# Sharing PSUM by single banks and pairs, with gates on ScalarE and new paces, in a planned attention and FFN kernel

## Chip, core and metric

One core of a Trainium2 chip runs the whole kernel in one launch. The metric is the device time of one execution in microseconds (us). The engines are TensorE (PE in the profile), VectorE (DVE), ScalarE (ACT), GpSimd (POOL) and SyncE (SP), which issues nearly all DMAs here. Each runs its own instructions in order and waits on semaphores for the others.

## What is computed

```python
def _A_ref(x, wqkv, w_phi, wo):                    # x: 1 x 2048 x 640, 32 heads of 20
    qkv = (x @ wqkv).reshape(B, S, 3, H, Dh).transpose(2, 0, 3, 1, 4)
    q, k, v = qkv[0], qkv[1], qkv[2]
    pq = einsum("bhsd,hdf->bhsf", q, w_phi)
    pk = einsum("bhsd,hdf->bhsf", k, w_phi)
    phi_q = concatenate([softmax(pq), softmax(-pq)], axis=-1)
    phi_k = concatenate([softmax(pk), softmax(-pk)], axis=-1)
    kv = einsum("bhsf,bhsd->bhfd", phi_k, v)
    z  = einsum("bhsf->bhf", phi_k)
    o  = einsum("bhqf,bhfd->bhqd", phi_q, kv) / (einsum("bhqf,bhf->bhq", phi_q, z) + 1e-6)
    return o.transpose(0, 2, 1, 3).reshape(B, S, D) @ wo
def _B_ref(x, w_gate, w_up, w_down):               # inner width 1728
    return (silu(x @ w_gate) * (x @ w_up)) @ w_down
g = sigmoid((x * gate_w).sum(-1, keepdims=True))
out = g * _A_ref(x, ...) + (1 - g) * _B_ref(x, ...)
```

All data are bf16. The attention is linear, so keys and values of all 2048 tokens must be summed before the first query tile can be finished.

## The kernel before

The 2048 tokens are 16 tiles of 128 (index `t`) in 4 batches of 512 (index `bt`). Work is cut into tasks, each for one engine.

- **Premultiply** (`premult`, task `pre`): the feature weights are folded into the key and query weights, in five pieces each. A piece is six small matmuls into two PSUM banks, and ACT or DVE copies it to `wqk` (L722 on DVE, the helper L412 on ACT).
- **Values and gates** (`vtile`, tasks `v`, `vcp`, `gtan`): one tile of values with one more column, the gate's logit. ACT copies the values and takes a tanh of half the logit into `gtan`. After every fourth tile the task `gs` makes `gs[:, 0]` = 0.5 gtan + 0.5 and `gs[:, 1]` = 0.5 - 0.5 gtan for the four tiles, with two TENSOR_SCALAR on DVE (L755, L757).
- **Features** (`features`; `p1` for keys through `ktile`, `p0` for queries through `qtile`): 10 matmuls into two banks. Then come the row maximum (L799), the minimum (L803) and two subtractions (L807, L811) on DVE, the Exp on ACT, sums (L822) and reciprocal (L826) on DVE, and the normalisation on POOL (L832). The banks are free behind L811. The pool `pp` lets two such tiles hold PSUM at a time.
- **Key-value sums** (`kvpart`): per batch two halves, each into one bank, added up on DVE.
- **Query tiles** (`qtile`): the features are transposed by DMA, multiplied with the sums (`num`), divided (`den`, L914, and `o`), transposed by DMA again and multiplied with `wo`.
- **FFN** (`ffn`, `ffn_tail`, `ffn_head`): for each block `k` of 128 inner columns and each batch, 5 matmuls `gate` and 5 `up` of 512 columns. ACT makes a tanh of the gate's half and a copy of the up part (`us`), DVE combines tanh and gate (`stt`, L579), and POOL multiplies by the up part (`hmul`, L585). Block 13 is half as wide and has both parts in one bank. `down` then takes 28 matmuls for a tile; it needs all 14 blocks of its batch.
- **Output** (`finish`, `finals`): the branch that comes first is scaled by its gate into `xsb`, the other is scaled and added, and SP stores the tile.

The order of instructions is not written by hand. `_Plan.run` is a list scheduler that runs when the kernel is built: for each engine it takes, at the modelled time, the first task by priority whose dependencies have ended, whose earliest time (`hold`) has come and whose buffers are free. What it emits is fixed, and the chip executes it in that order. Keys have priority 3, values 4, queries 5 and FFN blocks and `down` 10 and up (a smaller number goes first), so the FFN fills what the attention leaves. The costs that it plans with stand in the `add` calls (0.75 us for L799, L803, L807 and L811, 1.44 for L822, 0.47 for L826, 0.59 for L579, and 0.08 more between dependent instructions of one engine).

PSUM has 8 banks of 512 fp32 columns. Before, the plan hands them out as four pairs (`"ps": 4`), for every task alike: an FFN block holds a pair from its first matmul until `stt` is done, and a half of the key-value sums or the warm-up holds a pair of which it uses one bank.

The paces: key tile `t` starts no earlier than 26.0 + 6.19 t, query tile `t` no earlier than 120.1 + 8.21 t, and piece `m` of the key weights no earlier than 21.4 + 1.1 m (all us on the plan's clock). `D_AFTER` says behind how many FFN blocks of the next batch the first `down` of a batch is put in the priorities.

Of the kernel before, what the change touches and what calls it, by code (L numbers as in the profile page):

```python
# [6 lines left out]
P = 128  # L7
# [7 lines left out]
NK = 14  # L15
# [191 lines left out]
class _Task:  # L207
    __slots__ = ("eng", "cost", "lat", "fn", "deps", "prio", "acq", "rel", "end", "seq", "name", "stop", "after", "land", "hold", "slack")
# [20 lines left out]
class _Plan:  # L229
# [16 lines left out]

    def run(self):
        left = {e: [] for e in self.LAT}
        for t in sorted(self.tasks, key=lambda t: (t.prio, t.seq)):
            left[t.eng].append(t)  # L250
        busy = {e: 0.8 for e in self.LAT}
        releases = []
        now = 0.0
        n = len(self.tasks)
        times = {0.8} | {t.hold for t in self.tasks if t.hold > 0.8}
        while n:
            if not times:
                names = [t.name for e in left for t in left[e]][:12]
                raise RuntimeError("plan is stuck: %s" % names)
            now = min(times)  # L260
            times.discard(now)
            for r in [r for r in releases if r[0] <= now]:
                releases.remove(r)
                self.free[r[1]].append(r[2])
                self.free[r[1]].sort()
# [37 lines left out]
def _build(  # L303
# [75 lines left out]
    plan = _Plan({"ps": 4, "phi": NPHI, "st": 3, "eT": 2, "ob": 2, "oT": 2, "us": 3, "dn": 2, "xb": 2, "pp": 2})  # L379
    add = plan.add  # L380

    def bank(i, j, c0, c1, r0=0, r1=P):
        return ps[r0:r1, (2 * i + j) * 512 + c0:(2 * i + j) * 512 + c1]

# [158 lines left out]
    def warm():  # L543
        z = us[:, 0, :]
        mms(acc(bank(wctx["ps"], 1, 0, 512), [(us[:, 0, 0:P], z)] * 9))
    warm_t = add("pe", 3.84, warm, deps=[zero], prio=-10, acq=[("ps", wctx, "ps")], rel=[("ps", wctx, "ps")], name="warm")


# [11 lines left out]
    def ffn_tail(bt, k, ctx, last, n_after):  # L560
        hb = bt % 2
        rows = P if k < 13 else 64
        hap = hT[0:rows, hb, k, :]

        def gap():
            return bank(ctx["ps"], 0, 0, 512, 0, rows)

        def uap():
            return bank(ctx["ps"], 1, 0, 512) if k < 13 else bank(ctx["ps"], 0, 0, 512, 64, P)
# [12 lines left out]

        def mult():
            u_ = usa()
            poolop(lambda: pool.tensor_tensor(hap, hap, u_, ALU.mult), [hap, u_], [hap])  # L585
        mult_t[bt, k] = add("pool", 1.11, mult, deps=[t2, t3], prio=0, rel=[("us", ctx, "us")], name="hmul")

    def ffn(bt, k, rank):
# [4 lines left out]
        if k == 13:  # L593
            one = add("pe", _mm(*[512] * 5), lambda: mms(acc(bank(ctx["ps"], 0, 0, 512),
                      [(wg[:, c, 1664:1792], xT[:, c, tsl]) for c in range(5)])),
                      deps=before + [xl[bt], wgl[NPC], wul[NPC]], prio=rank, acq=[("ps", ctx, "ps")], name="gu")
            ffn_tail(bt, k, ctx, (one, one), 0)
            return
        g_ = add("pe", _mm(*[512] * 5), lambda: mms(acc(bank(ctx["ps"], 0, 0, 512),
                 [(wg[:, c, P * k:P * k + P], xT[:, c, tsl]) for c in range(5)])),  # L600
                 deps=before + [xl[bt], wgl[w_]], prio=rank, acq=[("ps", ctx, "ps")], name="gate")
        u_ = add("pe", _mm(*[512] * 5), lambda: mms(acc(bank(ctx["ps"], 1, 0, 512),
                 [(wu[:, c, P * k:P * k + P], xT[:, c, tsl]) for c in range(5)])),
                 deps=[wul[w_]], prio=0.0, name="up")
# [3 lines left out]
    def ffn_head():  # L608
# [4 lines left out]
        for c0, c1 in ((0, 2), (2, 4), (4, 5)):  # L613
            for j, (w, wl) in enumerate(((wg, wgl), (wu, wul))):
                def fn(c0=c0, c1=c1, j=j, w=w):
                    mms([(bank(cs[k]["ps"], j, 0, 512), w[:, c, P * k:P * k + P], xT[:, c, tsl], c == 0, c == 4)
                         for c in range(c0, c1) for k in range(2)])
                last = add("pe", _mm(*[512] * (2 * (c1 - c0))), fn, deps=[xs[0][c1 - 1], wl[0]], prio=-5,
                           acq=[("ps", cs[0], "ps"), ("ps", cs[1], "ps")] if c0 == 0 and j == 0 else (), name="head")
# [18 lines left out]
    def finish(t, which, ctx, dep):  # L638
        sc = gs[:, 0 if which == "a" else 1, t:t + 1]
        x_ = xsb[:, t, :]  # L640
        rel = [("ps", ctx, "ps")]
# [34 lines left out]
    def down(bt, u, rank):  # L676
# [8 lines left out]
        hold = {"deps": [mult_t[bt, k] for k in range(NK)] + wd_l, "prio": rank, "acq": [("ps", ctx, "ps")], "name": "down"}  # L685
# [12 lines left out]
    def premult(which, wT_l, prio, step=0.0, at=0.0):  # L698
        ev = []
        for m in range(5):  # L700
# [14 lines left out]
            t1 = add("pe", 0.4, fn, deps=[wT_l] + wbd_t, prio=prio + step * m, acq=[("ps", ctx, "ps")], name="pre")  # L715
            t1.hold = at + 1.1 * m if at else 0.0

            def ev_fn(m=m, ctx=ctx):
# [4 lines left out]
                else:  # L723
                    actop(o_, i_, ACTF.Copy)
            ev.append(add("dve" if which and m % 2 else "act", 0.73 if which and m % 2 else 0.6, ev_fn, deps=[t1], prio=-1,
                          rel=[("ps", ctx, "ps")], name="prev"))
# [6 lines left out]
    def vtile(t, prio):  # L733
# [6 lines left out]
        def fn():  # L740
# [3 lines left out]
                 acq=[("ps", ctx, "ps")], name="v")  # L744
# [4 lines left out]
                 deps=[c_], prio=0.4, rel=[("ps", ctx, "ps")], name="gtan")  # L749
        v_t[t] = c_  # L750
        if t % 4 == 3:
            q = slice(4 * bt, 4 * bt + 4)

            def gsf():
                dveop(lambda: dve.tensor_scalar(gs[:, 0, q], gtan[:, q], 0.5, 0.5, op0=ALU.mult, op1=ALU.add),  # L755
                      [gtan[:, q]], [gs[:, 0, q]])
                dveop(lambda: dve.tensor_scalar(gs[:, 1, q], gtan[:, q], -0.5, 0.5, op0=ALU.mult, op1=ALU.add),  # L757
                      [gtan[:, q]], [gs[:, 1, q]])
            gs_t[bt] = add("dve", 0.3, gsf, deps=[g_], prio=2, name="gs")
# [7 lines left out]
    def features(t, which, wq_l, prio, ctx):  # L767
# [6 lines left out]
        def fn():  # L774
# [4 lines left out]
                 acq=[("ps", ctx, "ps"), ("phi", ctx, "phi"), ("st", ctx, "st"), ("pp", ctx, "pp")], name="p" + str(which))  # L779
# [36 lines left out]
        a4 = add("dve", 0.75, f_sn, deps=[a2, a3], prio=age, rel=[("ps", ctx, "ps"), ("pp", ctx, "pp")], name="sub")  # L816
# [16 lines left out]
        b1 = add("dve", 1.44, f_sm, deps=[x1], prio=age, name="sum")  # L833
# [9 lines left out]
    def kvpart(bt, half, prio):  # L843
# [4 lines left out]
        def fn():  # L848
            grp = []
            for g in range(g0, g1):  # L850
                c0, c1 = WIN * g, min(WIN * g + WIN, VW)
                o_ = bank(ctx["ps"], 0, c0 - WIN * g0, c1 - WIN * g0)
                for i in range(4):
# [4 lines left out]
                 prio=prio, acq=[("ps", ctx, "ps")],  # L858
# [6 lines left out]
        p_ = lambda: bank(ctx["ps"], 0, 0, v1_ - v0)  # L865
# [14 lines left out]
        if bt < NBT - 1:  # L880
            kva_t[half] = add("dve", 0.48, evac, deps=[m_, kva_t.get(half)], prio=1.5, rel=[("ps", ctx, "ps")], name="kva")
# [3 lines left out]
        else:  # L885
            kvs_t[half] = add("dve", 0.95, masked, deps=[m_, kva_t[half]] + mask_t, prio=1.4, rel=[("ps", ctx, "ps")], name="kvs")
# [3 lines left out]
    def qtile(t, prio):  # L890
# [34 lines left out]
        d2 = add("dve", 0.73, f_o, deps=[d1], prio=1.2, rel=[("ps", c2, "ps"), ("dn", c2, "dn")], name="o")  # L925
# [9 lines left out]
        a_ = add("pe", _mm(*([512] * 5 + [128] * 5)), wof, deps=[tO, wo_l], prio=1.5, acq=[("ps", c3, "ps")],  # L935
# [90 lines left out]
```

## Time and profile before

| | |
|---|---|
| median of 3 runs | 292.12 us (291.95 to 292.25) |
| profiled execution | 291.88 us |
| its span, first to last instruction | 289.7 us |
| granted TensorE clock | 1.000 |
| busy: PE, DVE, POOL, ACT | 281.7, 226.0, 166.9, 145.1 us |
| HBM read, written | 8.30 MB, 2.62 MB |

The page divides the span into 40 slices and gives each engine's busy share in tenths. It follows the chain of work that ended last backwards from the last instruction. Other views list instructions in order of time, with the idle time of the engine just before each and what ended it, or give the busy time in chosen stretches. Matmuls overlap in the pipeline, so one row's duration is longer than the distance to the next row. Some matmul records are missing in a trace; weight loads (PEld) are all there: 2065 of them stand against 2027 matmul records here.

### The profile page before, as it was taken

What the parts mean: (1) busy time and instruction counts of PE and PEld (TensorE: products, weight loads), DVE (VectorE), ACT (ScalarE), POOL (GpSimd) and SP (SyncE); (2) the same over time, 40 slices, a digit from 0 to 9 for tenths busy, and PEclk for the clock granted to TensorE, in tenths of its full rate; (3) what the DMA queues carried; (4) which work ended last, traced back from release to release, by engine and by line L of the source; (5) the groups of instructions that cost most, each with busy time, mean ns of one, the idle gap of its engine ahead of it and who ended that gap; (6) DMA issues with size and microseconds to landing.
All of it is one profiled execution on the core that took longest, in us unless ns stands there. A gap on an engine that the chain in (4) does not pass through costs nothing.

```text
span 289.7 us, 5139 instructions
## 1 busy us (share of the span) xinstructions
PE 281.7 (97%) x2027; PEld 151.7 (52%) x2065; DVE 226.0 (78%) x325; ACT 145.1 (50%) x214; POOL 166.9 (58%) x131
## 2 busy tenths in 40 slices
PE   7999998999999999999999999999999999999996
PEld 2445554555555446555655555555455555445554
DVE  1234798999899998989999887888998987872112
ACT  2546465665865744444463634555665455564110
POOL 5396134576575467574377575787697455666100
PEclk9999999999999999999999999999999999999999
DMA  8999998000000000000053444523443533322211
GB/s 181 226 230 323 248 267 265 1 5 0 2 0 2 0 2 0 2 0 0 2 101 75 94 97 96 111 65 85 75 79 68 118 76 73 72 46 52 70 45 45
DMA packets 65415, 23.90 MB, mean 82 GB/s; under 512 B 53936, under 2 KB 65392, under 8 KB 65392
## 3 DMA queue, kind: packets, MB, share of 16 engines
q1 hardware_dynamic: 64736, 23.58, 36.0%
q8 instruction: 16, 0.26, 0.4%
q10 hardware_dynamic: 656, 0.00, 0.1%
q14 instruction: 7, 0.06, 0.1%
HBM read 8.30 MB, written 2.62 MB: 38 GB/s over the span
## 4 chain that ended last, share of the span: by engine, by line
PE 85%; DVE 5%; POOL 3%; SPq 2%; issue 2%; DMA 1%; ACT 1%; ACTq 0%; POOLq 0%
PE ps L402 85%; SPq L430 2%; POOL hT L585 2%; DMA wph<-in_A_w_phi_dram 1%; DVE sm L822 1%; DVE mx L799 1%; DVE phi L807 1%; DVE phi L811 1%; DVE mn L803 1%; POOL wbd L520 1%; POOL wbd L523 1%; DVE gs L755 0%; POOL wbd L519 0%; ACT wqk L412 0%; ACT us L412 0%
## 5 line engine op out<-in xcount | busy, mean ns | idle before, releaser
L832 POOL TENSOR_TENSOR phi<-phi,rc 128x1320 bf16<-128x1320 bf16 x32 | 77.6, 2426 | 48.0 <-DVE rc L826 47.9
L585 POOL TENSOR_TENSOR hT<-hT,us 128x512 bf16<-128x512 bf16 (+1 forms) x56 | 64.2, 1155 | 35.7 <-DVE hT L579 30.2
L402 PE MATMUL ps<-xT,wg 128*128 128x512 bf16 x268 | 67.0, 379 | 0.9 <-ACT wqk L412 0.3
L402 PE MATMUL ps<-xT,wu 128*128 128x512 bf16 x254 | 64.3, 379 | 0.7 <-DMA wu<-in_B_w_up_dram 0.3
L402 PE MATMUL ps<-wd,hT 128*128 128x128 bf16 (+1 forms) x441 | 61.9, 298 | 0.4
L822 DVE TENSOR_REDUCE sm<-phi 128x66 f32<-128x1320 bf16 x32 | 48.7, 1521 | 11.5 <-ACT phi L412 11.2
L412 ACT ACTIVATE hT<-ps 128x512 bf16<-128x512 f32 (+1 forms) x56 | 33.2, 595 | 40.5 <-PE ps L402 40.4
L412 ACT ACTIVATE phi<-phi 128x1320 bf16<-128x1320 bf16 x32 | 41.6, 1301 | 23.1 <-DVE phi L811 23.0
L579 DVE SCALAR_TENSOR_TENSOR hT<-hT,ps 128x512 bf16<-128x512 bf16 (+1 forms) x56 | 37.5, 674 | 19.3 <-ACT hT L412 19.3
L402 PE MATMUL ps<-wqk,xT 128*128 128x512 bf16 (+2 forms) x315 | 48.0, 299 | 1.6 <-DVE phi L811 1.3
L402 PEld LDWEIGHTS ps<-wd,hT 128*128 128x128 bf16 x448 | 35.0, 98 | 27.4
L402 PEld LDWEIGHTS ps<-xT,wu 128*128 128x128 bf16 x260 | 25.4, 98 | 31.2 <-DMA wu<-in_B_w_up_dram 0.8
L412 ACT ACTIVATE us<-ps 128x512 bf16<-128x512 f32 (+1 forms) x56 | 33.3, 596 | 16.4 <-PE ps L402 14.9
L402 PEld LDWEIGHTS ps<-xT,wg 128*128 128x128 bf16 x280 | 25.5, 98 | 26.8 <-issue 0.9
L402 PEld LDWEIGHTS ps<-wqk,xT 128*128 128x128 bf16 x320 | 26.5, 98 | 23.2 <-DVE phi L811 1.5
L799 DVE TENSOR_REDUCE mx<-ps 128x33 f32<-128x660 f32 x32 | 26.3, 822 | 4.1 <-PE ps L402 3.7
L811 DVE TENSOR_TENSOR phi<-mn,ps 128x660 bf16<-128x660 f32 x32 | 26.5, 829 | 0.6
L803 DVE TENSOR_REDUCE mn<-ps 128x33 f32<-128x660 f32 x32 | 26.4, 824 | 0.0
L807 DVE TENSOR_TENSOR phi<-ps,mx 128x660 bf16<-128x660 f32 x32 | 26.2, 819 | 0.0
L671 POOL TENSOR_TENSOR xsb<-xsb,xb 128x640 bf16<-128x640 bf16 x12 | 16.7, 1396 | 14.2 <-ACT xb L412 14.2
L412 ACT ACTIVATE xsb<-ps,gs 128x640 bf16<-128x640 f32 x16 | 12.6, 790 | 23.0 <-PE ps L402 23.0
L402 PE MATMUL ps<-wo,oT 128*128 128x512 bf16 (+1 forms) x154 | 22.9, 296 | 0.4
(45 smaller groups left out, 184.6 us busy)
## 6 DMA issues: line engine op xcount, KB each, us to landing
out_dram<-xsb SPq DMA_DIRECT2D x15, 160.0 KB, 1.9
wd<-in_B_w_down_dram SPq DMA_DIRECT2D x1, 2080.0 KB, 9.4
wg<-in_B_w_gate_dram SPq DMA_DIRECT2D x3, 320.0 KB, 3.8
wu<-in_B_w_up_dram SPq DMA_DIRECT2D x3, 320.0 KB, 4.6
wvg<-in_A_wqkv_dram SPq DMA_DIRECT2D x1, 800.0 KB, 7.6
wo<-in_A_wo_dram SPq DMA_DIRECT2D x1, 800.0 KB, 10.2
wg<-in_B_w_gate_dram SPq DMA_DIRECT2D x1, 640.0 KB, 4.6
wu<-in_B_w_up_dram SPq DMA_DIRECT2D x1, 640.0 KB, 5.8
```

Of the source, the lines that this page charges most:

```text
L402: last = pe.matmul(o, lhsT=l, rhs=r, start=st, stop=sp_, skip_group_check=True)
L412: run("act", lambda: act.activation(o, i, func, scale=scale), reads=reads, writes=[o])
L430: fn = (lambda: eobj.dma_start(dst, src, transpose=True)) if transpose else (lambda: eobj.dma_start(dst, src))
L579: dveop(lambda: dve.scalar_tensor_tensor(out=hap, in0=hap, scalar=1.0, in1=g_, op0=ALU.add, op1=ALU.mult), [hap, g_], [hap])
L585: poolop(lambda: pool.tensor_tensor(hap, hap, u_, ALU.mult), [hap, u_], [hap])
L671: poolop(lambda: pool.tensor_tensor(x_, x_, b_, ALU.add), [x_, b_], [x_])
L799: dveop(lambda: dve.tensor_reduce(a, b, AX.X, ALU.max), [b], [a])
L803: dveop(lambda: dve.tensor_reduce(a, b, AX.X, ALU.min), [b], [a])
L807: dveop(lambda: dve.tensor_tensor(o_, a, b, ALU.subtract), [a, mx[:, ctx["st"], :]], [o_])
L811: dveop(lambda: dve.tensor_tensor(o_, a, b, ALU.subtract), [b, mn[:, ctx["st"], :]], [o_])
L822: dveop(lambda: dve.tensor_reduce(a, b, AX.X, ALU.add), [b], [a])
L832: poolop(lambda: pool.tensor_tensor(a, a, b, ALU.mult), [a, r], [a])
```

## The change

- The pool `ps` of four pairs becomes a pool `bank` of eight banks. A task asks for a `pair` (an even bank and its neighbour) or for single banks. A single bank is taken first where the neighbour is in use already. FFN `gate` and `up` take a bank each, the up bank is given back when ACT has copied it (`us`) and the gate bank after `stt`; `stt` no longer depends on `us`, except in block 13. Key-value sums and the warm-up take one bank; features, values, `pre`, `num`, `wo` and `down` take a pair.
- The task `gs` moves from DVE to ACT: two activations Copy with scale 0.5 or -0.5 and bias 0.5.
- The pieces of the key weights are held at 21.0 + 2.2 m.
- Key tiles are held at 26.0 + 5.70 t, query tiles at 118.6 + 8.46 t, and `D_AFTER` goes from 3 to 1.
- Two planned costs change: `sum` from 1.44 to 1.45 and `num` by 0.03.

```diff
+    def pairs(self):
+        f = self.free["bank"]
+        return [i for i in f if i % 2 == 0 and i + 1 in f]
+
+    def room(self, p, n):
+        if p == "pair":
+            return len(self.pairs()) >= n
+        return len(self.free[p]) >= n
+
+    def take(self, p):
+        if p == "pair":
+            i = self.pairs()[0]
+            self.free["bank"].remove(i)
+            self.free["bank"].remove(i + 1)
+            return i // 2
+        if p == "bank":
+            f = self.free[p]
+            i = min(f, key=lambda b: (b ^ 1 in f, b))
+            f.remove(i)
+            return i
+        return self.free[p].pop(0)
...
-                        if any(not self.free[p] for p, _, _ in t.acq):
+                        if not all(self.room(p, n_) for p, n_ in t.need):
                             continue
                         for p, ctx, key in t.acq:
-                            ctx[key] = self.free[p].pop(0)
+                            ctx[key] = self.take(p)
...
-    plan = _Plan({"ps": 4, "phi": NPHI, ...
+    plan = _Plan({"bank": 8, "phi": NPHI, ...
...
         t2 = add("act", 0.49, lambda: actop(usa(), uap(), ACTF.Copy, scale=0.5), deps=[last[1]], prio=0.1,
-                 acq=[("us", ctx, "us")], name="us")
+                 acq=[("us", ctx, "us")], rel=[("bank", ctx, "u")] if k < 13 else (), name="us")
...
-        t3 = add("dve", 0.59, stt, deps=[t1, t2], prio=0, rel=[("ps", ctx, "ps")], name="stt")
+        t3 = add("dve", 0.59, stt, deps=[t1, t2] if k == 13 else [t1], prio=0, rel=[("bank", ctx, "g")], name="stt")
...
-    K_AT, K_EACH, Q_AT, Q_EACH = 26.0, 6.19, 120.1, 8.21
+    K_AT, K_EACH, Q_AT, Q_EACH = 26.0, 5.70, 118.6, 8.46
     PRE_Q = 10.10
-    PRE_AT = 21.4
-    D_AFTER = 3
+    PRE_EACH = 2.2
+    PRE_AT = 21.0
+    D_AFTER = 1
...
-            t1.hold = at + 1.1 * m if at else 0.0
+            t1.hold = at + PRE_EACH * m if at else 0.0
...
             def gsf():
-                dveop(lambda: dve.tensor_scalar(gs[:, 0, q], gtan[:, q], 0.5, 0.5, op0=ALU.mult, op1=ALU.add),
-                      [gtan[:, q]], [gs[:, 0, q]])
-                dveop(lambda: dve.tensor_scalar(gs[:, 1, q], gtan[:, q], -0.5, 0.5, op0=ALU.mult, op1=ALU.add),
-                      [gtan[:, q]], [gs[:, 1, q]])
-            gs_t[bt] = add("dve", 0.3, gsf, deps=[g_], prio=2, name="gs")
+                for w, a in ((0, 0.5), (1, -0.5)):
+                    run("act", lambda w=w, a=a: act.activation(gs[:, w, q], gtan[:, q], ACTF.Copy, scale=a, bias=0.5),
+                        reads=[gtan[:, q]], writes=[gs[:, w, q]])
+            gs_t[bt] = add("act", 0.2, gsf, deps=[g_], prio=2, name="gs")
...
-        b1 = add("dve", 1.44, f_sm, deps=[x1], prio=age, name="sum")
+        b1 = add("dve", 1.45, f_sm, deps=[x1], prio=age, name="sum")
...
-                 prio=prio, acq=[("ps", ctx, "ps")],
+                 prio=prio, acq=[("bank", ctx, "ps")],
                  rel=[("phi", kctx[4 * bt + i], "phi") for i in range(4)] if half else (), name="kv")
...
-        m_ = add("pe", _mm(*[WIN] * (NG + 1)), num, deps=[tT, kvs_t[0], kvs_t[1]], prio=1, rel=[("eT", ctx, "eT")],
-                 acq=[("ps", c2, "ps"), ("dn", c2, "dn"), ("ob", c2, "ob")], name="num")
+        m_ = add("pe", _mm(*[WIN] * (NG + 1)) + 0.03, num, deps=[tT, kvs_t[0], kvs_t[1]], prio=1, rel=[("eT", ctx, "eT")],
+                 acq=[("pair", c2, "ps"), ("dn", c2, "dn"), ("ob", c2, "ob")], name="num")
```

More of the change, by code (lines that the diff above doesn't have):

```diff
@@ L207 @@
 class _Task:
-    __slots__ = ("eng", "cost", "lat", "fn", "deps", "prio", "acq", "rel", "end", "seq", "name", "stop", "after", "land", "hold", "slack")
+    __slots__ = ("eng", "cost", "lat", "fn", "deps", "prio", "acq", "rel", "end", "seq", "name", "stop", "after", "land", "hold", "slack", "need")
     def __init__(self, eng, cost, fn, deps, prio, lat, acq, rel, seq, name):
@@ L245, in add, with give @@
         return t
+    def pairs(self):
[17 more added lines that the diff above has]
+        return self.free[p].pop(0)
+    def give(self, p, v):
+        self.free["bank" if p == "pair" else p] += [2 * v, 2 * v + 1] if p == "pair" else [v]
+        self.free["bank" if p == "pair" else p].sort()
     def run(self):
+        for t in self.tasks:
+            names = [p for p, _, _ in t.acq]
+            t.need = [(p, names.count(p)) for p in set(names)]
         left = {e: [] for e in self.LAT}
@@ L377, in _build @@
     out2 = out[0]
-    plan = _Plan({"ps": 4, "phi": NPHI, "st": 3, "eT": 2, "ob": 2, "oT": 2, "us": 3, "dn": 2, "xb": 2, "pp": 2})
+    plan = _Plan({"bank": 8, "phi": NPHI, "st": 3, "eT": 2, "ob": 2, "oT": 2, "us": 3, "dn": 2, "xb": 2, "pp": 2})
     add = plan.add
@@ L544, in warm @@
         z = us[:, 0, :]
-        mms(acc(bank(wctx["ps"], 1, 0, 512), [(us[:, 0, 0:P], z)] * 9))
-    warm_t = add("pe", 3.84, warm, deps=[zero], prio=-10, acq=[("ps", wctx, "ps")], rel=[("ps", wctx, "ps")], name="warm")
+        mms(acc(one(wctx["ps"], 0, 512), [(us[:, 0, 0:P], z)] * 9))
+    warm_t = add("pe", 3.84, warm, deps=[zero], prio=-10, acq=[("bank", wctx, "ps")], rel=[("bank", wctx, "ps")], name="warm")
     gate_t = {}
@@ L565, in gap @@
         def gap():
-            return bank(ctx["ps"], 0, 0, 512, 0, rows)
+            return one(ctx["g"], 0, 512, 0, rows)
         def uap():
-            return bank(ctx["ps"], 1, 0, 512) if k < 13 else bank(ctx["ps"], 0, 0, 512, 64, P)
+            return one(ctx["u"], 0, 512) if k < 13 else one(ctx["g"], 0, 512, 64, P)
         def usa():
@@ L615, in fn @@
                 def fn(c0=c0, c1=c1, j=j, w=w):
-                    mms([(bank(cs[k]["ps"], j, 0, 512), w[:, c, P * k:P * k + P], xT[:, c, tsl], c == 0, c == 4)
+                    mms([(one(cs[k]["gu"[j]], 0, 512), w[:, c, P * k:P * k + P], xT[:, c, tsl], c == 0, c == 4)
                          for c in range(c0, c1) for k in range(2)])
                 last = add("pe", _mm(*[512] * (2 * (c1 - c0))), fn, deps=[xs[0][c1 - 1], wl[0]], prio=-5,
-                           acq=[("ps", cs[0], "ps"), ("ps", cs[1], "ps")] if c0 == 0 and j == 0 else (), name="head")
+                           acq=[("bank", cs[k], "gu"[j]) for k in range(2)] if c0 == 0 else (), name="head")
                 last.after = before
@@ L684, in part @@
                        [(hT[:, hb, k, tk], wd[:, k, 512:D] if j else wd[:, k, 0:512]) for k in range(NK)])
-        hold = {"deps": [mult_t[bt, k] for k in range(NK)] + wd_l, "prio": rank, "acq": [("ps", ctx, "ps")], "name": "down"}
+        hold = {"deps": [mult_t[bt, k] for k in range(NK)] + wd_l, "prio": rank, "acq": [("pair", ctx, "ps")], "name": "down"}
         if t < NT - 1:
@@ L748, in vtile @@
         g_ = add("act", 0.06, lambda: actop(gtan[:, t:t + 1], bank(ctx["ps"], 1, 128, 129), ACTF.Tanh, scale=0.5),
-                 deps=[c_], prio=0.4, rel=[("ps", ctx, "ps")], name="gtan")
+                 deps=[c_], prio=0.4, rel=[("pair", ctx, "ps")], name="gtan")
         v_t[t] = c_
@@ L778, in features @@
         m_ = add("pe", _mm(*([512] * 5 + [148] + [128] * 4)), fn, deps=[xl[bt]] + wq_l, prio=prio,
-                 acq=[("ps", ctx, "ps"), ("phi", ctx, "phi"), ("st", ctx, "st"), ("pp", ctx, "pp")], name="p" + str(which))
+                 acq=[("pair", ctx, "ps"), ("phi", ctx, "phi"), ("st", ctx, "st"), ("pp", ctx, "pp")], name="p" + str(which))
         m_.hold = K_AT + K_EACH * t if which else Q_AT + Q_EACH * t
@@ L851, in fn @@
                 c0, c1 = WIN * g, min(WIN * g + WIN, VW)
-                o_ = bank(ctx["ps"], 0, c0 - WIN * g0, c1 - WIN * g0)
+                o_ = one(ctx["ps"], c0 - WIN * g0, c1 - WIN * g0)
                 for i in range(4):
@@ L863, in kvpart @@
         ka = kvacc[:, v0:v1_]
-        p_ = lambda: bank(ctx["ps"], 0, 0, v1_ - v0)
+        p_ = lambda: one(ctx["ps"], 0, v1_ - v0)
         km = kvm[:, 0:v1_ - v0]
@@ L885, in kvpart @@
         else:
[L886 removed]
+            kvs_t[half] = add("dve", 0.95, masked, deps=[m_, kva_t[half]] + mask_t, prio=1.4, rel=[("bank", ctx, "ps")], name="kvs")
     kva_t = {}
```

35 lines of the change are left out of this document (18 added, 17 removed).

## The prediction

> **What bounds the kernel now.** I read the page first, for the busiest engine and the chain that ended last.
>
> ```profile
> span 289.7 us, 5139 instructions
> PE 281.7 (97%) x2027; PEld 151.7 (52%) x2065; DVE 226.0 (78%) x325; ACT 145.1 (50%) x214; POOL 166.9 (58%) x131
> PE   7999998999999999999999999999999999999996
> PEclk9999999999999999999999999999999999999999
> PE 85%; DVE 5%; POOL 3%; SPq 2%; issue 2%; DMA 1%; ACT 1%; ACTq 0%; POOLq 0%
> ```
>
> PE is busy in nine tenths or more of nearly every slice, its clock is full, and 85% of the chain lies on it. The change takes no matmul away, so PE's 281.7 us stay. Only the 289.7 - 281.7 = 8.0 us in which PE idles can be won. The order of PE's work costs nothing as long as something is ready, so the question for each edit is whether it removes or makes a wait of PE.
>
> A busy PE could still be a slow PE, so I looked at a stretch without waits in PE's list in order of time. An FFN half of five 512-column matmuls:
>
> ```profile
> 18.84 1.24 PE L402 MATMUL ps<-xT,wg 128*128 128x512 bf16 x5
> 19.92 1.24 PE L402 MATMUL ps<-xT,wu 128*128 128x512 bf16 x5
> ```
>
> They start 1.08 us apart, 216 ns for each matmul. A row is 1.24 - 1.08 = 0.16 us longer than its distance to the next, so an idle time printed behind such a row is 0.16 us too short. The Trainium skill (Perfetto Trace Analysis, "Identifying the Most-Contended Engine") says that the matmul row's busy share is a bad measure of headroom and that MFU and the weight loads' share are better; by the 52% of PEld there would be much room. It also states (TensorE: Matmul & The Clock Gate) N / 2.4 GHz + about 2.5 ns between warm matmuls, 215.7 ns for 512 columns, which the 216 ns here agree with; so the trace decides for no room.
>
> Next, PE's waits, and the rows at which they happen:
>
> ```profile
> PE ps L402 <- DVE phi L811: 1.3, 1, 1.3
> PE ps L402 <- DVE us L422: 1.3, 1, 1.3
> PE ps L402 <- ACT wqk L412: 0.7, 2, 0.4
> PE ps L402 <- DMA wu<-in_B_w_up_dram: 0.3, 1, 0.3
> ```
> ```profile
> 23.16 1.11 PE L402 MATMUL ps<-wbd,wqT 128*128 128x140 bf16 x18
> 24.69 0.47 PE L402 MATMUL ps<-wbd,wqT 128*128 128x140 bf16 x6 [0.43 <-ACT wqk L412]
> 27.16 0.48 PE L402 MATMUL ps<-wbd,wqT 128*128 128x140 bf16 x6
> 29.64 1.53 PE L402 MATMUL ps<-wqk,xT 128*128 128x512 bf16 x10
> 39.20 5.63 PE L402 MATMUL ps<-wvg,xT 128*128 128x512 bf16 x39
> 46.13 1.54 PE L402 MATMUL ps<-wqk,xT 128*128 128x512 bf16 x10 [1.31 <-DVE phi L811]
> 87.45 1.02 PE L402 MATMUL ps<-xT,wg 128*128 128x512 bf16 x4 [0.28 <-ACT wqk L412]
> ...
> 27.86 0.70 ACT L412 ACTIVATE wqk<-ps 128x640 bf16<-128x640 f32 x1
> ```
>
> This is the whole account. The start (the wait for L422, the wait for `wu`) and the tail behind the last matmul are not touched. Left are one wait of key tile 3 at 44.8 us, one of the fourth premultiply piece at 24.3, and one at 87.2. With 0.16 added, they cost 1.47, 0.59 and 0.44. The last row has four matmuls where a half has five, so one record of 0.22 is missing there, and the true gap is 0.22. Together 2.28 us.
>
> **Gates on ACT.** Why was key tile 3 late? It needs the banks that L811 frees, so I followed DVE back.
>
> ```profile
> 38.54 0.78 DVE L811 TENSOR_TENSOR phi<-mn,ps 128x660 bf16<-128x660 f32 x1
> 39.24 1.92 DVE L755 TENSOR_SCALAR gs<-gtan 128x4 f32<-128x4 f32 x1
> 41.07 0.16 DVE L757 TENSOR_SCALAR gs<-gtan 128x4 f32<-128x4 f32 x1
> 41.14 0.83 DVE L799 TENSOR_REDUCE mx<-ps 128x33 f32<-128x660 f32 x1
> 45.30 0.77 DVE L811 TENSOR_TENSOR phi<-mn,ps 128x660 bf16<-128x660 f32 x1
> 38.63 0.17 ACT L412 ACTIVATE gtan<-ps 128x1 f32<-128x1 f32 x1
> 38.70 2.43 POOL L832 TENSOR_TENSOR phi<-phi,rc 128x1320 bf16<-128x1320 bf16 x1 [6.97 <-DVE rc L826]
> L755 DVE TENSOR_SCALAR gs<-gtan x4: 158/162/1916, 39.2 to 96.8; 128x4 f32<-128x4 f32 x4
> ```
>
> Four numbers per partition took 1.92 us once and 0.16 in the median. Its input was ready at 38.80. It ended at 41.16, when POOL's normalisation ended (38.70 + 2.43 = 41.13). So I read it as DVE held off by POOL for 1.92 - 0.16 = 1.76 us. Here the Trainium skill bears on the case (SBUF — State Buffer, "Who interferes with whom"): `tensor_scalar` between SBUF operands can run in a two-port mode that needs the port pair shared with GpSimd, whoever comes second waits for the whole instruction, and ACT waits on nobody; the trace's 1.92 against 0.16 agrees, and by it the loss is gone with the instruction.
>
> From 41.14 to 46.07 DVE runs without a pause into the L811 that PE waits for. Without the two gate instructions (41.14 - 39.24 = 1.90 us) that L811 ends at 44.17, before PE is free at 44.67. So the whole 1.47 goes. What is late next there? Nothing on PE: the cover is 0.5 us, and if that is eaten, 0.1 us late costs 0.1 us. On ACT the change adds 8 activations; the nearest row is the one-column `gtan` at 0.17, so at most 8 x 0.17 = 1.4 us, on an engine that idles half of that stretch (5.64 busy of 10 us, below). Queued behind them are Exp and value copies, which come 0.3 us later at four places. Zero, if DVE has a backlog; up to 4 x 0.3 us if not.
>
> **Pieces of wk further apart.** Before, three pieces ran back to back and the fourth waited for a copy to free a pair. At 2.2 us apart an FFN block (2 x 1.08 = 2.16) fits between two, and the copy (0.70) is long done: -0.59. The price is a later start of the keys. The last piece moves from 27.16 to at least 29.8, and key tile 0 follows its copy. That ended at 28.56, 1.40 behind the piece's start, and the tile came at 29.64, 2.48 behind it; so now between 31.2 and 32.3. PE does FFN meanwhile, whose weights are there. DVE starts its key work 1.5 to 2.6 us later, and has 1.9 us less to do by tile 3. Zero on PE.
>
> **Single banks.** FFN blocks hold the up bank shorter (not until `stt`), and key-value sums and the warm-up one bank instead of two. No priority changes, and a single bank is taken beside a used one, so pairs stay whole more often. I take -0.22 for the wait at 87.2, as an FFN block now needs one free bank to begin; between 0 and -0.22.
>
> **Paces.** Can DVE follow key tiles 5.70 us apart?
>
> ```profile
> 40.00:50.00 10.00, 8.59 (x58) 4.65 (x58) 8.56 (x13) 5.64 (x12) 3.81 (x3) 1.00 0.91 300
> 50.00:60.00 10.00, 9.95 (x63) 5.12 (x62) 9.93 (x14) 6.29 (x10) 6.90 (x5) 1.00 0.01 3
> 60.00:80.00 20.00, 19.84 (x164) 11.23 (x166) 18.81 (x27) 13.58 (x23) 12.82 (x8) 1.00 0.00 1
> 80.00:100.00 20.00, 19.61 (x159) 10.96 (x160) 19.65 (x29) 12.75 (x22) 11.77 (x7) 1.00 0.00 1
> 100.00:120.00 20.00, 19.83 (x157) 10.92 (x159) 18.56 (x27) 8.98 (x12) 14.41 (x11) 1.00 0.00 1
> 52.48 0.84 DVE L811 TENSOR_TENSOR phi<-mn,ps 128x660 bf16<-128x660 f32 x1
> 58.67 0.84 DVE L811 TENSOR_TENSOR phi<-mn,ps 128x660 bf16<-128x660 f32 x1
> ```
>
> The third busy time is DVE's: 9.93 + 18.81 + 19.65 + 18.56 = 66.95 of the 70 us from 50 to 120, 3.05 spare. By the plan's costs a key tile takes 4 x 0.75 + 1.44 + 0.47 = 4.9 us of DVE. At 5.70 instead of 6.19, 70 us hold 12.3 tiles instead of 11.3, one more, 4.9 us; so the pace can't be held and the tiles slide to what DVE gives. That is no loss by itself: a key tile whose banks are not free in the plan is passed over for an FFN block. It becomes one if the plan takes DVE for faster than it is, since the chip then waits where the plan did not. From 52.48 to 58.67 DVE is full: 8 instructions in 6.19 us, for which the plan has 4 x 0.75 + 2 x 0.59 + 1.44 + 0.47 = 6.09, plus 0.08 for one dependence: 6.17. An error of 0.02 for a tile, 0.3 us over 16. I take zero, bounds 0 and +0.3.
>
> Query tile 15 may start at 118.6 + 15 x 8.46 = 245.5 instead of 243.25, 2.25 later.
>
> ```profile
> 244.57 1.53 PE L402 MATMUL ps<-wqk,xT 128*128 128x512 bf16 x10
> 261.35 3.97 PE L402 MATMUL ps<-wd,hT 128*128 128x512 bf16 x28
> 274.49 1.52 PE L402 MATMUL ps<-wo,oT 128*128 128x512 bf16 x10
> 275.84 11.57 PE L402 MATMUL ps<-wd,hT 128*128 128x512 bf16 x82
> ```
>
> Tile 15 came at 244.57 and its `wo` ran at 274.49 to 276.0. Only the last `down` (28 matmuls, 3.97 us of the group that ends at 287.41, so from 283.4) needs its result. With 2.25 more it is there at about 278.3 plus a store of some 0.8, over 4 us early. Zero. `D_AFTER` puts a `down` behind two FFN blocks (4.3 us) instead of four; the plan places it only when it takes the products for done. Zero, and the slower rival covers its misjudging.
>
> **The sum.** 1.47 + 0.59 + 0.22 = 2.28 off the profiled 291.88 (span 289.7 and 2.18 around it) is 289.60. The median of the runs is 292.12, 0.24 above the profiled one, so the forecast is 292.12 - 2.28 = **289.8 us**. The least is this minus the `wu` wait (0.30 + 0.16), if the start happens to shift, and the lower half of the spread of runs (0.17): 289.2.
>
> **The rivals.**
> ```profile
> 140.00:160.00 20.00, 19.84 (x150) 10.68 (x153) 19.83 (x32) 8.52 (x14) 12.79 (x8) 1.00 0.37 70
> L826 DVE RECIPROCAL rc<-sm x32: 507/556/566, 38.1 to 256.2; 128x66 f32<-128x66 f32 x32
> ```
>
> *First use.* The 1.92 us instruction is also the first TENSOR_SCALAR on DVE. Were that the cause, it would move to the next such, L914 of the first `den`, at about 150 us, where DVE is full (19.83 of 20). PE would lose there up to the 1.47 again: 291.3. For it: the other three were short. Against it: the end matches POOL's end, and the reciprocal, whose first use comes in the same stretch, shows no such thing (its longest of 32 is 0.566). The same 290.3 to 291.5 results if only one of the two large waits goes.
> *Moved wait.* Small waits eat the gain: 13 key tiles at 0.16 us make 2.1, hence no change, 292.0.
> *Slower: the paces take the margin away.* With the hold at 6.19 a key tile came a little after DVE was free for it. At 5.70 each is placed at the moment the plan frees a pair, so that every lateness of DVE, ACT or POOL (whose engine also feeds `down`) stops PE. If each of the 13 tiles from the fourth on costs what the smallest such row shows, 0.28, that is 3.6 us, net 1.4 slower: 293.5. It decides from 2.28 / 13 = 0.18 us per tile. For it: DVE is over-asked, and no slack is left. Against it: the plan's DVE costs fit the trace to 0.02 a tile, and between 60 and 80 us, where DVE was 94% busy, PE was held up nowhere.
>
> **How the numbers follow.** Forecast 0.66 (289.2 to 290.3), a part lost 0.13 (290.3 to 291.5), no change 0.05, slower 0.16. A measurement here can tell 0.2% (0.58 us). Faster takes the first two less a bit at the edge: 0.78; same 0.06; slower 0.16. The range 289.2 to 292.0 leaves out the slower rival and little else.
>
> **What would show it.** Right: no DVE row of the gates, none of `den` over its usual length, no row on PE with an idle time over 0.3 us between 10 and 280 us, PE's busy time again 281 to 282, a span near 287.4, key tile 0 at 31.2 to 32.3 us. Wrong in the first rival's way: a `den` of about 2 us. In the slower one's: many waits of PE for L811, L826 or POOL between 45 and 130 us, or before a `down`.

## The result and the profile after

| | before | after |
|---|---|---|
| median (runs) | 292.08 us (291.75 to 292.25, 6) | 289.44 us (289.26 to 289.99, 6) |
| ratio, 95% interval | | 0.9912 (0.9900 to 0.9925) |
| profiled execution, span | 291.88, 289.7 us | 289.35, 287.2 us |

The change takes 2.64 us off, 0.9%. The forecast was 289.8. First the page of the changed kernel: span, busy times, PE and its clock in 40 slices, and the chain by engine.

```profile
span 287.2 us, 5141 instructions
PE 281.4 (98%) x2028; PEld 152.0 (53%) x2065; DVE 224.6 (78%) x317; ACT 144.5 (50%) x222; POOL 166.7 (58%) x131
PE   8999999999999999999999999999999999999996
PEclk9999999999999999999999999999999999999999
PE 89%; DVE 9%; issue 1%
```

PE's busy time is the same (281.7 before), its idle time has gone from 8.0 to 5.8 us. Of its waits one line is left, the one at the start:

```profile
PE ps L434 <- DVE us L454: 1.3, 1, 1.3
```

PE in order of time, around the premultiply pieces (`wbd,wqT`) and the first key tiles:

```profile
23.13 0.79 PE L434 MATMUL ps<-wbd,wqT 128*128 128x140 bf16 x12
...
25.92 0.48 PE L434 MATMUL ps<-wbd,wqT 128*128 128x140 bf16 x6
...
28.39 0.48 PE L434 MATMUL ps<-wbd,wqT 128*128 128x140 bf16 x6
...
30.07 0.48 PE L434 MATMUL ps<-wbd,wqT 128*128 128x140 bf16 x6
...
31.75 2.90 PE L434 MATMUL ps<-wqk,xT 128*128 128x512 bf16 x20
...
46.25 1.53 PE L434 MATMUL ps<-wqk,xT 128*128 128x512 bf16 x10
```

The first two pieces still run back to back (12 matmuls at 23.13), the other three stand apart. Key tile 0 comes at 31.75 (29.64 before), and key tile 3 at 46.25 carries no idle time. The gates, from the tile's own view and from ACT's list, and the first `den` (L946, L914 before):

```profile
L789 ACT ACTIVATE gs<-gtan x8: 189/205/224, 41.1 to 98.3; 128x4 f32<-128x4 f32 x8
L946 DVE TENSOR_SCALAR dn<-ps x16: 127/188/192, 144.2 to 268.3; 128x32 f32<-128x32 f32 x16
41.09 0.32 ACT L789 ACTIVATE gs<-gtan 128x4 f32<-128x4 f32 x2
45.09 0.30 ACT L789 ACTIVATE gs<-gtan 128x4 f32<-128x4 f32 x2
```

All eight are short, the second pair beside a running normalisation on POOL (from 44.90 on), and no `den` is over 0.192. DVE's share of the key stretch (third busy time) and the end of PE's list:

```profile
50.00:60.00 10.00, 9.95 (x63) 5.22 (x63) 10.00 (x15) 7.26 (x11) 5.86 (x4) 1.00 0.00 1
60.00:80.00 20.00, 19.83 (x164) 11.20 (x166) 19.93 (x27) 12.75 (x24) 13.38 (x8) 1.00 0.01 2
80.00:100.00 20.00, 19.83 (x163) 11.14 (x165) 19.90 (x28) 12.48 (x23) 13.06 (x9) 1.00 0.00 1
100.00:120.00 20.00, 19.84 (x161) 11.15 (x163) 18.91 (x26) 7.64 (x10) 13.93 (x9) 1.00 0.01 2
113.57 1.53 PE L434 MATMUL ps<-wqk,xT 128*128 128x512 bf16 x10
...
244.27 1.53 PE L434 MATMUL ps<-wqk,xT 128*128 128x512 bf16 x10
...
275.73 1.52 PE L434 MATMUL ps<-wo,oT 128*128 128x512 bf16 x9
277.09 7.77 PE L434 MATMUL ps<-wd,hT 128*128 128x512 bf16 x56
```

DVE is busy for 68.74 of these 70 us (66.95 before), and yet PE waits for it nowhere. The last key tile comes at 113.57, the last query tile at 244.27 (244.57 before).

### The profile page after: what moved, and what is told of

The parts are those of the page before. It is cut to its first block, busy times and chain, and to the rows that moved or that the text cites. A ratio compares the mean times of both kernels' runs of the same rounds, so it can differ in the third digit from the quotient of the medians.

```text
span 287.2 us, 5141 instructions
## 1 busy us (share of the span) xinstructions
PE 281.4 (98%) x2028; PEld 152.0 (53%) x2065; DVE 224.6 (78%) x317; ACT 144.5 (50%) x222; POOL 166.7 (58%) x131
## 4 chain that ended last, share of the span: by engine, by line
PE 89%; DVE 9%; issue 1%
PE ps L434 89%; DVE sm L854 2%; DVE hT L611 1%; DVE phi L839 1%; DVE mx L831 1%; DVE mn L835 1%; DVE phi L843 1%; DVE rc L858 1%; DVE kvacc L904 0%; DVE xsb L690 0%; DVE us L454 0%
## 5 line engine op out<-in xcount | busy, mean ns | idle before, releaser
L434 PE MATMUL ps<-wd,hT 128*128 128x512 bf16 (+1 forms) x443 | 62.5, 298 | 0.3
L434 PE MATMUL ps<-wqk,xT 128*128 128x512 bf16 (+2 forms) x313 | 47.4, 298 | 0.4
```

The costliest lines, as they stand in the source:

```text
L434: last = pe.matmul(o, lhsT=l, rhs=r, start=st, stop=sp_, skip_group_check=True)
```

## The experiments

Ten further kernels were run, one of them twice, and the change once more, in three groups of four. The kernels of a group shared a chip and the runs of the kernel before; the first two groups ran on one chip, the third on another. Ratios are to the kernel before in the same group (292.1 us each time). The kernels with pairs keep the two planned costs of the kernel before (`sum` and `num`), those with banks have the new ones; no run takes these costs apart from the sharing.

**Gates alone.** The two activations of the change in place of the two DVE instructions, nothing else.

```diff
...
-            gs_t[bt] = add("dve", 0.3, gsf, deps=[g_], prio=2, name="gs")
+            gs_t[bt] = add("act", 0.2, gsf, deps=[g_], prio=2, name="gs")
```

> Only the gates move to ACT; pairs, pieces and paces as before. Theory (GpSimd's normalisation held the gate instruction off, 1.76 us of DVE, and PE lost 1.47 at key tile 3): that wait is gone, the waits of the premultiply piece at 24.3 us and at 87.2 stay, time 292.1 - 1.5 = 290.6. Rival first use (the first TENSOR_SCALAR on DVE is slow): the first `den` takes about 1.9 us and PE loses up to the same again, 290.6 to 292.1. Rival paces and banks (they make the gain, the gates matter little): 291.9 or more.

Measured: 290.60 us, ratio 0.9946 (0.9934 to 0.9959). That is 1.5 less, with the wait for key tile 3 gone and the two waits for `wqk` still there (0.7 us in two). The gates' term of the sum stands.

**Sharing alone.** Gates on DVE, old pieces and paces, single banks.

```diff
-    plan = _Plan({"ps": 4, ...
+    plan = _Plan({"bank": 8, ...
...
```

> Only the sharing by banks and pairs; gates on DVE, pieces 1.1 us apart, old paces. Theory: the waits for a pair at 24.3 and 87.2 us go (0.59 + 0.22 = 0.8), the gate instruction is planned at the same place beside a normalisation and stays long, so 291.3. Rival paces and banks: the banks alone bring most of the 2.6 us, 290 or less.

Measured: 292.38 us, ratio 1.0009 (1.0000 to 1.0017). No gain, against both expectations. The waits for `wqk` were gone, but others had come. DVE's list (the gates' rows), POOL's list, and PE's waits:

```profile
39.05 1.92 DVE L788 TENSOR_SCALAR gs<-gtan 128x4 f32<-128x4 f32 x1
...
45.93 1.04 DVE L788 TENSOR_SCALAR gs<-gtan 128x4 f32<-128x4 f32 x1
...
75.48 0.16 DVE L788 TENSOR_SCALAR gs<-gtan 128x4 f32<-128x4 f32 x1
...
98.94 2.19 DVE L788 TENSOR_SCALAR gs<-gtan 128x4 f32<-128x4 f32 x1
```
```profile
38.51 2.42 POOL L865 TENSOR_TENSOR phi<-phi,rc 128x1320 bf16<-128x1320 bf16 x1 [6.97 <-DVE rc L859]
44.51 2.43 POOL L865 TENSOR_TENSOR phi<-phi,rc 128x1320 bf16<-128x1320 bf16 x1 [3.58 <-DVE rc L859]
...
98.67 2.42 POOL L865 TENSOR_TENSOR phi<-phi,rc 128x1320 bf16<-128x1320 bf16 x1 [4.99 <-DVE rc L859]
```
```profile
PE ps L434 <- DVE hT L611: 1.4, 3, 0.6
...
PE ps L434 <- DVE phi L844: 0.5, 2, 0.3
```

Three of four gate instructions began behind a normalisation on POOL, and each ended where that ended: 40.97 against 40.93, 46.97 against 46.94, 101.13 against 101.09. The one at 75.48 found POOL idle and took 0.16. DVE lost 1.76 + 0.88 + 2.03 = 4.7 us instead of 1.76. PE's printed waits behind the start are 1.9 us, all for DVE, where the kernel before had 2.0, so what the sharing won is gone. The same kernel with its gates on ACT, told below, has none of these waits and takes 289.87 and 289.69 us: beside single banks the gates on ACT are worth 2.6 us. The hold-off is shown; how often it strikes is an accident of the order.

**The change with its gates back on DVE.**

```diff
...
-            gs_t[bt] = add("act", 0.2, gsf, deps=[g_], prio=2, name="gs")
+            gs_t[bt] = add("dve", 0.3, gsf, deps=[g_], prio=2, name="gs")
```

> The changed kernel with the gates back on DVE. Theory: what counts is whether a gate instruction falls into a normalisation on POOL. In the changed kernel the gates' inputs were ready at 41.2 and 45.1 us and the normalisations ran from 42.29 to 44.72 and from 44.90 to 47.33, so the first pair should be short (0.16) and the second be held for about 1 to 2 us; key tile 4 was due at 49.6 only, so PE loses between 0 and 1 us: 289.4 to 290.4. Rival first use: the first of the four is the long one (1.9) and the second is short. Rival paces and banks: 289.4, nothing lost.

Measured: 289.94 us, ratio 0.9928 (0.9916 to 0.9940), and the rows came as the theory had them. DVE, POOL, and the PE row that paid:

```profile
41.08 0.16 DVE L788 TENSOR_SCALAR gs<-gtan 128x4 f32<-128x4 f32 x1
...
45.75 1.16 DVE L788 TENSOR_SCALAR gs<-gtan 128x4 f32<-128x4 f32 x1
```
```profile
41.86 2.42 POOL L865 TENSOR_TENSOR phi<-phi,rc 128x1320 bf16<-128x1320 bf16 x1 [11.20 <-DVE rc L859]
44.46 2.42 POOL L865 TENSOR_TENSOR phi<-phi,rc 128x1320 bf16<-128x1320 bf16 x1 [0.18 <-DVE rc L859]
```
```profile
52.03 1.24 PE L434 MATMUL ps<-xT,wg 128*128 128x512 bf16 x5 [0.24 <-DVE hT L611]
```

The first TENSOR_SCALAR is short and the second long, so the first-use rival falls. The 1.00 us of DVE costs PE 0.4 at this row (0.24 and the 0.16 that a printed gap leaves out). In the changed order the gates on ACT are worth less than in the order before, 0.2 to 0.5 us (289.94 against 289.75 and 289.44) instead of 1.5; the intervals of these ratios overlap, so the row is the better evidence.

**Gates on DVE, column by column**, in the kernel before:

```diff
...
+                for i in range(4 * bt, 4 * bt + 4):
+                    for w, a in ((0, 0.5), (1, -0.5)):
+                        o_, i_ = gs[:, w, i:i + 1], gtan[:, i:i + 1]
+                        dveop(lambda o_=o_, i_=i_, a=a: dve.tensor_scalar(o_, i_, a, 0.5, op0=ALU.mult, op1=ALU.add), [i_], [o_])
```

> The kernel before with the gates left on DVE, each TENSOR_SCALAR of four columns cut into four of one column. Theory (a TENSOR_SCALAR between SBUF operands that runs in a two-port mode waits for the end of the POOL instruction; one element per partition can't be split over two ports): all 32 short, about 0.16 each and some 0.06 apart, PE's wait for key tile 3 gone, 290.6 to 290.9. Rival (any TENSOR_SCALAR from SBUF to SBUF waits for POOL): the first of the 32 takes 1.9 us as before, 292.1 or more.

Measured: 291.32 us, ratio 0.9972 (0.9963 to 0.9981). The 32 instructions, the first eight of them, and POOL at that time:

```profile
L758 DVE TENSOR_SCALAR gs<-gtan x32: 140/142/146, 39.7 to 96.8; 128x1 f32<-128x1 f32 x32
39.72 0.56 DVE L758 TENSOR_SCALAR gs<-gtan 128x1 f32<-128x1 f32 x8
39.18 2.42 POOL L832 TENSOR_TENSOR phi<-phi,rc 128x1320 bf16<-128x1320 bf16 x1 [6.98 <-DVE rc L826]
```

Same operation, same tiles, same place inside a normalisation, and all eight done in 0.56 us: what is held off is the form of four columns, not the TENSOR_SCALAR as such. The Trainium skill (SBUF — State Buffer, "Who interferes with whom") states that a `tensor_scalar` contends with GpSimd where it can enter a two-port mode. The Trainium skill also gives the condition for that mode (VectorE: DVE Perf Modes, "What auto-detection actually checks"): source and destination in SBUF, with outermost dimensions other than one that are both even or equal. Four columns meet this. That a single column has nothing to split over two ports is a reading of the condition, and the run agrees with it; the ports themselves stand in no trace.

The gain is smaller than expected (0.8 instead of 1.2 to 1.5 us). In the profiled execution the start is one reason: the row of up matmuls that begins at 15.60 in the kernel before begins at 16.08, 0.48 later. From that row on this kernel is 0.91 us faster than the one before, and the run of the gates alone is 1.57 faster (there the row stands at 15.96). Of the 0.66 between them PE's rows show some 0.6 in three small gaps that no wait list names, of 0.3, 0.1 and 0.2 us at 52, 58 and 85 us. The eight instructions take 0.48 us of DVE at four places, which fits, but that they make these gaps is not shown.

**Everything but the sharing.** Gates on ACT, wide pieces and new paces, with four pairs.

```diff
-    plan = _Plan({"bank": 8, ...
+    plan = _Plan({"ps": 4, ...
...
```

> The changed kernel with pairs alone (four pairs for every task): gates on ACT, pieces 2.2 us apart, new paces. Theory that the sum of the forecast is made of (gates and pieces carry 2.06 of 2.28, the sharing 0.22): 289.4 + 0.2 = 289.7. Rival: the new paces and the wider pieces need the single banks; with pairs a feature tile and a piece hold PSUM from the FFN, the order that the planner makes has holes on PE of 0.2 to 0.7 us between 58 and 98 us that add up to some 2.5, and the time is near 291.9, with waits of PE for ACT's copies to `wqk` and for DVE.

Measured: 292.67 us, ratio 1.0021 (1.0012 to 1.0030): slower than the kernel before. The sum's 289.7 falls, and the time is 0.8 above the rival's. PE's list shows two of the holes, both behind a query piece:

```profile
57.47 0.48 PE L402 MATMUL ps<-wbd,wqT 128*128 128x140 bf16 x6
58.60 1.24 PE L402 MATMUL ps<-xT,wg 128*128 128x512 bf16 x5 [0.65 <-DVE hT L579]
...
87.93 0.47 PE L402 MATMUL ps<-wbd,wqT 128*128 128x140 bf16 x6
88.95 2.68 PE L402 MATMUL ps<-wvg,xT 128*128 128x512 bf16 x19 [0.55 <-DVE kvacc L873]
```

An FFN block or a value tile needs a pair, and by the releasers none is free: PE starts when an `stt` (L579) gives back the pair of an FFN block, or the adding up (L873) that of a key-value half, which uses one bank of its two. The rival's waits for ACT's copies are not in PE's list. The printed waits behind the start, with 0.16 added to each, make some 2.1 of the 3.1 us between this profiled execution and that of the change; the rest is not in the list. So the sharing is worth 292.67 - 289.44 = 3.2 us in this order, where the forecast had 0.22. Three kernels take the four edits apart.

**Gates and sharing, gates and pieces, gates and paces.**

Each adds one part of the change to the kernel with the gates alone: the sharing (run twice),

```diff
-    plan = _Plan({"ps": 4, ...
+    plan = _Plan({"bank": 8, ...
...
```

> Gates on ACT and the sharing by banks; pieces 1.1 us apart and the old paces. New theory (the edits are not additive: with single banks the planner's order has no hole on PE under either set of paces and pieces, and the gates' hold-off is the only thing left): 289.4 to 289.7, as the whole change. Rival (new paces or wider pieces carry a part of their own, the 0.59 of the forecast for the pieces): 290.0 or more, with a wait of PE at 24 us for the copies to `wqk`.

> Gates on ACT and sharing by banks, old pieces and paces, beside the changed kernel on the same chip. Theory (pieces and paces bring nothing once single banks are there): within 0.3 us of the changed kernel. Rival (they carry a part of their own): 0.4 us or more above it again, as 289.87 against 289.44 was on two chips.

or the pieces,

```diff
-            t1.hold = at + 1.1 * m if at else 0.0
+            t1.hold = at + 2.2 * m if at else 0.0
-    PRE_AT = 21.4
+    PRE_AT = 21.0
```

> Gates on ACT and pieces 2.2 us apart; pairs for every task and the old paces. The forecast's sum: 292.1 - 1.47 - 0.59 = 290.0. New theory: with pairs, later key pieces push the query pieces to where an FFN block, a feature tile and a piece need more pairs than there are; the planner's order has holes on PE of 0.7 and 1.0 us before key-value sums and 0.4 later, so 290.6 + 1.6 = 292.2.

or the paces:

```diff
-    K_AT, K_EACH, Q_AT, Q_EACH = 26.0, 6.19, 120.1, 8.21
-    D_AFTER = 3
+    K_AT, K_EACH, Q_AT, Q_EACH = 26.0, 5.70, 118.6, 8.46
+    D_AFTER = 1
```

> Gates on ACT and the new paces; pairs for every task and pieces 1.1 us apart. The forecast's sum (paces cost and bring nothing): 290.6. New theory: the paces alone, with pairs, give an order with holes on PE that add up to some 3 us, beginning at the query pieces and going on among the query tiles: 293 to 294.

The change itself was run again beside the second run of gates and sharing.

> The changed kernel unaltered, as the measure for the three others on this chip: 289.4, ratio 0.991.

Measured, with the runs told above:

| gates | PSUM | pieces | paces | median, us | ratio (95%) |
|---|---|---|---|---|---|
| ACT | pairs | old | old | 290.60 | 0.9946 (0.9934 to 0.9959) |
| ACT | banks | old | old | 289.87 | 0.9925 (0.9911 to 0.9938) |
| ACT | banks | old | old, again | 289.69 | 0.9919 (0.9906 to 0.9932) |
| ACT | pairs | new | old | 292.24 | 1.0004 (0.9995 to 1.0012) |
| ACT | pairs | old | new | 293.66 | 1.0055 (1.0042 to 1.0067) |
| ACT | pairs | new | new | 292.67 | 1.0021 (1.0012 to 1.0030) |
| ACT | banks | new | new, again | 289.75 | 0.9913 (0.9900 to 0.9926) |

Lines two and three are the kernel with nothing but gates and sharing, and the last is the whole change, which ran beside line three on one chip: 289.69 and 289.75. Pieces and paces bring nothing that the runs can tell once single banks are there. The first run of gates and sharing, 289.87, lay between the theory's range and the rival's, without the wait at 24 us that the rival asked for; beside the change the theory's 0.3 us hold. With pairs the pieces cost 1.6 and the paces 3.1 us over the 290.60, near what their new theories had, and both together 2.1. Here are rows that pay, first of gates and pieces with its one wait for a copy to `wqk`, and then of gates and paces:

```profile
PE ps L402 <- ACT wqk L412: 0.8, 1, 0.8
...
63.40 0.86 PE L402 MATMUL ps<-v,phi 128*128 128x63 bf16 x24 [0.75 <-DVE hT L579]
...
86.53 0.74 PE L402 MATMUL ps<-v,phi 128*128 128x63 bf16 x20 [0.80 <-ACT wqk L412]
```
```profile
60.55 0.74 PE L402 MATMUL ps<-v,phi 128*128 128x63 bf16 x20 [0.80 <-ACT wqk L412]
...
252.29 1.02 PE L402 MATMUL ps<-xT,wg 128*128 128x512 bf16 x4 [0.60 <-ACT xsb L412]
```

The first three stand right behind a query piece (at 62.17, 85.25 and 59.28). Each is a key-value sum that by the list waits for an instruction whose result it does not use, so it waits for the pair and not for data. The last stands among the query tiles. Gates and pieces has a single wait for `wqk`, the one at 86.53: wider pieces alone took away the wait at 24.3, as single banks alone do.

What stays joined in every run: the single banks, the earlier return of the up bank, the dropped dependency of `stt` and the two planned costs count as the sharing, and the two paces and `D_AFTER` as the paces.

**The start.** The profiled executions also differ by what PE waits for the first up weights (0 to 0.9 us), and not only between kernels: the two runs of gates and sharing have 0 and 0.6. Two versions of the changed kernel tried to win that. The second moves one load, the first moves `wgl[0]` in the same way as well:

```diff
-wul[0] = load("sp", wu[:, :, 0:256], usrc[:, :, 0:256], 6.7, -41)
+wul[0] = load("act", wu[:, :, 0:256], usrc[:, :, 0:256], 6.7, -41)
```

> The changed kernel with the first piece of the gate weights and of the up weights issued from ACT's queue, so that SP starts with the transposing loads of x. The runs so far differ by what PE waits for the first up weights (0 to 0.9 us). If the order of issue on SP sets this (0.46 for the gate weights, 1.31 for x, 0.57 for the up weights, one after the other): the first FFN matmul comes some 0.4 us earlier, the wait is gone, 288.6 to 289.1. If the transfers themselves set it, since the DMA engines are shared: 289.4, with the wait at another load (batch 1 of x at 14 us).

> The same with the first piece of the up weights alone on ACT's queue. If the issue sets the wait: the wait of PE for these weights is gone in every run, batch 0 of x comes no earlier, 289.0 to 289.3. If the transfers set it: 289.4, or up to 0.3 more because the first x shares the engines with them.

Measured: 291.88 us (290.12 to 293.39; ratio 0.9990, 0.9968 to 1.0012) with both loads on ACT's queue, 290.49 (289.84 to 291.93; 0.9953, 0.9937 to 0.9969) with one. Neither beats the change, and both lie above either of their expected ranges. The first FFN matmuls in PE's list and, behind them, the row of up matmuls from which on PE runs evenly, of the change again, of both loads and of one, and the latter row of the kernel before:

```profile
5.43 1.51 PE L434 MATMUL ps<-xT,wg 128*128 128x512 bf16 x4
...
16.00 1.24 PE L434 MATMUL ps<-xT,wu 128*128 128x512 bf16 x5
```
```profile
6.80 1.86 PE L434 MATMUL ps<-xT,wg 128*128 128x512 bf16 x4 [1.52 <-DMA xT<-in_A_x_dram]
...
17.86 1.24 PE L434 MATMUL ps<-xT,wu 128*128 128x512 bf16 x5
```
```profile
6.37 1.02 PE L434 MATMUL ps<-xT,wg 128*128 128x512 bf16 x4 [1.38 <-DMA xT<-in_A_x_dram]
...
16.08 1.24 PE L434 MATMUL ps<-xT,wu 128*128 128x512 bf16 x5
```
```profile
15.60 1.24 PE L402 MATMUL ps<-xT,wu 128*128 128x512 bf16 x5
```

In the first PE did not wait for x. With the weights issued beside it the first part of x lands later, by at least 1.4 us with both loads and 0.9 with one, and the wait for the up weights becomes a larger one for x, even where x was issued earlier (0.80 instead of 1.34). So the order of issue on SP does not set the start. That the transfers hold each other up fits the rows, but no run shows it apart. The profiled execution with one load is the fastest of its twelve, so it shows little of what the median lost.

The second rows tell how much of a profiled execution is its start. Beside those shown, this row stands at 15.57 in the first profiled execution of the change and at 15.59 and 15.90 in those of gates and sharing. With the distance from 15.60 taken off, the change takes 289.38 and 289.37 us, gates and sharing 289.45 and 289.43, and the two versions above 289.38 and 289.36. So what these two lose in their profiled executions is lost ahead of this row, and pieces and paces with single banks are worth at most 0.1 us.

## Why the prediction was right, and where it was not

The whole was right: PE is the bound, its matmuls stayed, and what could be won was its three waits. 2.28 us were named, the medians differ by 2.64 (the interval reaches from 2.2 to 2.9), and all three waits are gone. The profiled executions differ by 2.53, and behind the start by 2.50. The 0.2 above the sum lie within what the runs can't tell apart: gates alone 1.57 instead of 1.47, sharing 0.87 instead of the 0.81 of pieces and banks, pieces and paces at most 0.1. How the sum was shared out among the edits was not right, and that it came out all the same is in part luck.

The gates' step held in each part: POOL's normalisation as the cause (shown in three kernels, and by the column form), 1.47 us on PE (1.5 in the run of the gates alone), nothing late behind it, no move to `den`. On ACT the eight activations took 0.205 us in the median, 1.6 in all and not at most 1.4, and PE waited for none of it. What the step did not see is that its size hangs on the order: 1.5 with pairs, 2.6 beside single banks with the old paces, 0.2 to 0.5 in the changed order.

The step on the pieces was right about its one wait and wrong as a step. It gave -0.59 to their spacing, with zero for the later keys. The wait at 24.3 does go with the spacing alone. But added to the gates with pairs the pieces cost 1.6 us on balance: the order that the planner then makes stops PE behind two query pieces (0.75 and 0.80). I had looked at the five pieces that the pace holds and not at what it does to the order behind them. In the change the spacing adds nothing, since the kernel with banks and old pieces has no wait at 24.3 either.

The step on the banks was mis-sized: 0.22 where the runs show 290.60 - 289.78 = 0.8 with the old paces (289.78 is the mean of the two medians), just what I had split into 0.59 and 0.22, and 3.2 with the new ones. I priced it by the one wait that I could see and not by what the other edits would ask of PSUM.

The step on the paces had the right total for the wrong reason. I wrote that 5.70 can't be held and the tiles slide. They did not: from key tile 0 at 31.75 to key tile 15 at 113.57 are 5.45 us for a tile, and the last is 6.7 us earlier than before (120.28). The planner moved FFN blocks out of the way. DVE's `stt` take 9.43 us (14 of them) between 50 and 120, and took 10.83 (16), and DVE ran at 98%. The query tail, 2.25 us late in the forecast, did not start late: the last query tile came at 244.27, 0.3 earlier than before, and its `wo` 275.73 - 274.49 = 1.2 later. It had room, as forecast.

The slower rival did not come in this change, but its time did in another: paces with pairs took 293.66, where the rival had 293.5. The reason was the number of pairs and not DVE's lateness, so naming the price was luck.

The Trainium skill's rule on the shared ports (SBUF — State Buffer, "Who interferes with whom") decided rightly between POOL and first use. The measure of headroom that it prefers, the weight loads' share (Perfetto Trace Analysis, "Identifying the Most-Contended Engine"), stayed at 53% in a kernel whose PE idles 5.8 of 287.2 us, so the reading by distances between matmuls was the one that carried.

## What to carry to other kernels

Where an engine is full, price a change by that engine's waits, one row each, and ask of each edit whether another edit is what makes it harmless: with pairs the gates were worth -1.5 us, and on top of them the pieces cost 1.6 and the paces 3.1. The sharing alone brought nothing, with the gates it brought 0.8, and then pieces and paces cost nothing. When buffers are handed out in units larger than a task needs, a new pace can run out of them far from where the pace applies. A small instruction with a duration ten times its usual is worth a look at what the neighbouring engine did until that moment.

## What the runs showed that was not expected

- A TENSOR_SCALAR of 128 x 4 fp32 between SBUF tiles took 1.04 to 2.19 us when it began inside a POOL TENSOR_TENSOR, and ended 0.03 to 0.04 us behind it; as 128 x 1 it took 0.14 in the same place. The wait stands in the instruction's duration, not in the idle time before it, so no list of waits names it.
- Issuing one or two weight loads from a second queue made the first transposing load of x land at least 0.9 or 1.4 us later, and with two the runs spread over 3.3 us (290.12 to 293.39) where those of the change spread over 0.7.
